# Gated linear attention feeding a two-layer MLP: weight rows read from their third byte on, top parts rebuilt by ScalarE alone, and a new hand-written order

## The chip, the cores and the metric

One core of one Trainium2 chip runs the whole program. The metric is the device time of one execution in microseconds, median over runs.

## The reference

```python
# 4 batches, 8 heads, 768 tokens, head size 48, float32
state = alpha[t] * state + k[t] (outer) v[t]        # per head, 48 x 48
y[t]  = q[t] @ state
# x = y as 3072 tokens x 384 (all heads side by side)
h  = x @ w_in                     # 384 x 2048, float64 weights
sp = log(1 + exp(h))              # softplus
g  = h * erf(sp)
out = g @ w_out                   # 2048 x 384, float64 weights
```

The weights come as float64, eight bytes each. All matrix products are made as sums of products of a high part and a low part of each operand, to keep the accuracy of float32.

## The kernel before, in words

**Order.** Everything is unrolled. The string `ORDER` (lines 30 to 132) lists about 1600 steps; a step's name is its kind and its indices. `Queue` (line 195) chains each engine's instructions in just that order, so every engine (TensorE is `pe`, VectorE `dve`, ScalarE `act`, SyncE `sp`, GpSimd `pool`) works its own steps strictly one after another. All loads and stores are issued by SyncE.

**Attention.** 24 chunks of 128 rows (64 tokens of two batches). Per chunk n: loads `la lk lq lv` (alpha, k, q, v), two scans on VectorE `sb sa` and a reciprocal `rc`, scaled keys and queries `kk qq`, on TensorE a transpose `pn`, scores `ps`, outputs `qt` and `sv` into the PSUM tile `py`, and the state update `pu`, with `mk td ta` on VectorE (`ta` on ScalarE for the first two chunks) and `ic kn` on ScalarE (`kd` is `kn` on VectorE). Then the chunk's result is split for the MLP: `xh` (ScalarE) writes the high part `x_hi`; the low part `x_lo` comes from `xl`, one VectorE subtraction, or from `xp` (TensorE subtracts the high part in PSUM) and `xe` (ScalarE copies).

**MLP.** 12 blocks of 256 tokens; block n takes chunks 2n and 2n+1. Four groups g of 512 hidden columns, each in two halves. `hm_n_g_half` is 18 matmuls (three terms, high times high first, then the low weights, then the low x), `he` (ScalarE) or `hd` (VectorE) copies its PSUM bank to the tile `hs`. Then on ScalarE `u`, `n1 n2 n3`, `g`, on VectorE `ma mb z1 z2`; `ga` (ScalarE) or `gd` (VectorE) makes the high part, `gl` (VectorE) the low part, and `om_n_g_half` is 12 matmuls into `acc`. `oe` (ScalarE) or `ob` (VectorE) copies `acc` out, `od` stores. `u` and `g` need another activation table than `n1 n2 n3`, so ScalarE loads a table at each change of kind along its order.

**Weights.** 12 tiles of `w_in` (`wli_0` to `wli_11`, 128 x 512; `hm` of group g needs tiles 3g to 3g+2) and 16 of `w_out` (`wlo_f`, 128 x 384; `om_n_g_half` needs f = 4g+2half and the next). Class `Weight` (lines 635 to 696) turns the eight bytes of a number into a float32: `wl` loads the row shifted by three bytes, so that one 32-bit word holds bytes 3 to 6 (`low`) and the lowest byte of the next word is byte 7, sign and upper exponent (`rest`). `wr` (VectorE) shifts that byte to the top of a float32 `top`; `wd` (ScalarE) writes it as float16 into the upper half of the same word, which moves the exponent; `wa` (VectorE) shifts `low` by 5 and ors it in, giving `z`. Then `wh` (ScalarE; `wk` is the same on VectorE) makes the high part `hi`, and the low part comes from `wq` (VectorE subtracts) or from `wp` and `we` (TensorE subtracts in a PSUM bank, ScalarE copies).

**Tiles.** `w_in` loads take the ring `hs` (7 tiles), `w_out` loads the ring `s` (6 tiles, line 187), which the MLP's `u` also uses; `top` and `z` lie together in the ring `w` (4 tiles). A ring's tile is taken again when its last reader is done. `dw_n` issues n dummy products of the identity into a spare PSUM bank (two matmul records each); the first `dw` also clears two banks with four short ones.

Of the kernel before, what the change touches and what calls it, by code (L numbers as in the profile page):

```python
# [35 lines left out]
wdi_5 wri_7 wdi_8 qq_2 whi_6 lk_2 ic_2 wli_9 wai_5 wdi_7 hm_0_0_0 whi_5 kk_2 wli_10 hm_0_0_1 ta_1 he_0_0_0 qt_2 ps_2
wai_7 wli_11 la_3 wqi_5 he_0_0_1 pn_2 whi_7 wlo_0 wqi_6 kn_2 wai_8 lk_3 lq_3 wri_9 lv_2 hm_0_1_1 whi_8 wri_10 u_0_0
sb_3 wqi_8 wri_11 rc_3 wqi_7 he_0_1_1 hm_0_1_0 he_0_1_0 sa_3 mk_2 kk_3 wdi_9 qq_3 hm_0_2_0 wlo_7 sv_2 ps_3 wdi_10
wdi_11 he_0_2_0 pu_2 xh_2 wai_9 wro_7 whi_9 wdo_7 wai_10 pn_3 lv_3 ic_3 wai_11 whi_10 la_4 whi_11 wqi_9 lq_4 xp_2 kn_3
n1_0_0 mk_3 lk_4 xe_2 wqi_10 n2_0_0 wqi_11 td_3 hm_0_2_1 he_0_2_1 sb_4 hm_0_3_1 wro_0 ta_2 wlo_4 rc_4 qt_3 wdo_0 kk_4  # L40
he_0_3_1 pu_3 n3_0_0 sa_4 sv_3 xh_3 ta_3 pn_4 wao_7 wlo_1 la_5 wro_1 lq_5 wlo_2 xl_3 hm_0_3_0 who_7 kn_4 wao_0 qq_4
wdo_1 ma_0_0 he_0_3_0 lk_5 wao_1 hm_1_0_1 u_0_1 mb_0_0 td_4 hm_1_1_1 he_1_0_1 g_0_0 who_0 lv_5 he_1_1_1 lv_4 hm_1_0_0
sb_5 ps_4 wqo_7 qt_4 ic_4 n1_0_1 wro_2 hm_1_1_0 z1_0_0 n2_0_1 wqo_0 rc_5 mk_4 he_1_0_0 z2_0_0 wro_4 sa_5 wdo_2 wdo_4
la_6 who_1 he_1_1_0 ic_5 kk_5 td_5 hm_1_2_0 wao_4 hm_1_3_0 wqo_1 lk_6 sv_4 n3_0_1 wlo_11 ga_0_0_0 qq_5 ma_0_1 wao_2
ga_0_0_1 gl_0_0_0 ps_5 mb_0_1 sb_6 wlo_5 pu_4 g_0_1 xh_4 ta_4 xp_4 gl_0_0_1 who_2 mk_5 z1_0_1 he_1_2_0 wlo_6 wqo_2
om_0_0_0 he_1_3_0 pn_5 xe_4 u_0_2 rc_6 wro_5 hm_1_3_1 kk_6 n1_0_2 who_4 kn_5 om_0_0_1 wro_6 lq_6 he_1_3_1 wlo_9 wdo_5
n2_0_2 wdo_6 pn_6 sa_6 z2_0_1 qt_5 qq_6 pu_5 n3_0_2 lk_7 ga_0_1_0 wao_5 sv_5 ps_6 ga_0_1_1 xh_5 td_6 kn_6 la_7 lv_6
who_5 wao_6 xp_5 wqo_4 ic_6 xe_5 hm_1_2_1 wro_11 wlo_8 ma_0_2 gl_0_1_1 wdo_11 wao_11 hm_2_1_0 wko_6 wqo_5 wlo_12
gl_0_1_0 u_0_3 u_1_0 wro_9 ta_5 g_0_2 om_0_1_0 he_1_2_1 wqo_6 lq_7 hm_2_1_1 n1_0_3 mb_0_2 sb_7 z1_0_2 wdo_9 rc_7 mk_6
z2_0_2 wao_9 he_2_1_1 he_2_1_0 who_11 ic_7 sa_7 wlo_13 ga_0_2_1 om_0_1_1 wro_12 ga_0_2_0 kk_7 hm_2_0_0 qq_7 wqo_11  # L50
# [25 lines left out]
he_5_1_0 pu_12 n2_4_2 g_3_3 ma_4_1 sv_12 pn_13 xh_12 z1_3_3 mb_4_1 he_5_0_0 om_3_0_1 z2_3_3 g_4_1 z1_4_1 hm_5_0_1
la_14 g_4_0 gd_3_3_1 kn_13 z1_4_0 he_5_0_1 om_3_0_0 gd_3_3_0 sb_14 gl_3_3_0 xl_12 ic_13 lk_15 u_5_0 lv_13 rc_14 ta_12
sa_14 od_2_1 gl_3_3_1 u_4_3 mk_13 hm_5_1_1 om_3_3_0 kk_14 he_5_1_1 u_5_1 n1_4_3 n3_4_2 z2_4_0 hm_5_3_0 n1_5_0 qq_14
la_15 ma_4_2 om_3_3_1 n2_4_3 sv_13 ps_14 he_5_3_0 n1_5_1 pu_13 mb_4_2 qt_13 oe_3_0 pn_14 n3_4_3 z2_4_1 td_14 ic_14
oe_3_1 ga_4_0_0 ta_13 n2_5_0 sb_15 gl_4_0_0 hm_5_3_1 kn_14 he_5_3_1 om_4_0_0 gd_4_1_1 hm_5_2_0 ga_4_0_1 lq_15 xh_13  # L80
kk_15 gl_4_1_1 g_4_2 td_15 n2_5_1 om_4_1_1 rc_15 gl_4_0_1 n3_5_0 hm_5_2_1 lv_15 he_5_2_0 he_5_2_1 od_3_0 xl_13
om_4_0_1 n3_5_1 ma_4_3 sa_15 mb_4_3 gd_4_1_0 qq_15 z1_4_2 hm_6_0_1 u_5_2 mk_14 g_4_3 gl_4_1_0 la_16 om_4_1_0 ma_5_0
hm_6_0_0 g_5_0 z2_4_2 qt_14 z1_4_3 ps_15 lv_14 lk_16 u_5_3 sb_16 n1_5_3 mb_5_0 pu_14 he_6_0_0 n2_5_3 gd_4_2_0 od_3_1
sv_14 hd_6_0_1 ic_15 pn_15 xh_14 gl_4_2_0 z2_4_3 om_4_2_0 u_6_0 ma_5_1 rc_16 gd_4_2_1 ga_4_3_0 kd_15 g_5_1 ic_16
hm_6_2_1 lq_16 gl_4_2_1 om_4_2_1 gl_4_3_0 ga_4_3_1 mb_5_1 n3_5_3 kk_16 hd_6_2_1 z1_5_0 hm_6_2_0 sa_16 om_4_3_0
# [838 lines left out]
```

## Time and profile before

| | us |
|---|---|
| median of 3 runs (514.16 to 514.84) | 514.84 |
| the profiled execution | 513.94 |
| its span | 512.2 |
| busy: TensorE / VectorE / ScalarE | 502.5 / 481.5 / 461.5 |
| first matmul of the MLP (`hm_0_0_0`) starts | 26.95 |
| `om_4_0_0` starts | 235.40 |
| end of the last matmul | 506.9 |

A matmul shown as busy may be waiting in TensorE's pipeline, so the order of starts, not the busy share, tells where it stands still. All of the program's instructions go through the helper on line 203; the profile tells them apart by tiles: `warm` is a `dw`, `h` the PSUM bank of `hm`, `pn` and `wp`, `acc` an `om`, `w` with `s` or `hs` a weight or the MLP's `w`.

### The profile page before, as it was taken

What the parts mean: (1) busy time and instruction counts of PE and PEld (TensorE: products, weight loads), DVE (VectorE), ACT (ScalarE), POOL (GpSimd) and SP (SyncE); (2) the same over time, 40 slices, a digit from 0 to 9 for tenths busy, and PEclk for the clock granted to TensorE, in tenths of its full rate; (3) what the DMA queues carried; (4) which work ended last, traced back from release to release, by engine and by line L of the source; (5) the groups of instructions that cost most, each with busy time, mean ns of one, the idle gap of its engine ahead of it and who ended that gap; (6) DMA issues with size and microseconds to landing.
All of it is one profiled execution on the core that took longest, in us unless ns stands there. A gap on an engine that the chain in (4) does not pass through costs nothing.

```text
span 512.2 us, 16809 instructions
## 1 busy us (share of the span) xinstructions
PE 502.5 (98%) x7438; PEld 478.4 (93%) x7438; DVE 481.5 (94%) x659; ACT 461.5 (90%) x615; POOL 5.6 (1%) x39
## 2 busy tenths in 40 slices
...
GB/s 304 397 236 148 134 208 118 202 27 51 101 21 135 44 65 58 64 58 66 93 23 136 85 22 59 58 23 100 42 60 98 20 23 32 2 1 32 0 32 34
DMA packets 21387, 43.69 MB, mean 85 GB/s; under 512 B 2368, under 2 KB 5440, under 8 KB 21312
## 3 DMA queue, kind: packets, MB, share of 16 engines
...
## 4 chain that ended last, share of the span: by engine, by line
PE 68%; ACT 24%; DVE 3%; issue 3%; DMA 1%; SPq 0%; ACTq 0%
PE acc L203 31%; PE h__112 L203 15%; PE h__113 L203 13%; PE py L203 4%; ACT L203 4%; PE both L203 3%; ACT w__101 L203 2%; ACT w__99 L203 2%; ACT s__85 L203 1%; PE warm L203 1%; ACT w__100 L203 1%; ACT s__89 L203 1%; ACT s__88 L203 1%; ACT s__90 L203 1%; DMA s__85<-in_moe_w_out_dram 1%
## 5 line engine op out<-in xcount | busy, mean ns | idle before, releaser
L203 ACT ACT_TABLE_LOAD x74 | 94.9, 1283 | 2.1 <-PEq L878 0.9
L203 PE MATMUL acc<-wo_hi,gh__103 128*128 128x384 f32 x192 | 43.7, 339 | 0.0
L203 PE MATMUL acc<-wo_hi,gl__105 128*128 128x384 f32 x192 | 43.4, 338 | 0.0
L203 PE MATMUL acc<-wo_lo,gh__103 128*128 128x384 f32 x192 | 43.2, 337 | 0.0
L203 PE MATMUL acc<-wo_hi,gh__102 128*128 128x384 f32 x192 | 43.1, 344 | 0.0
L203 PE MATMUL acc<-wo_hi,gl__104 128*128 128x384 f32 x192 | 41.5, 338 | 0.3 <-DVE gl__104 L203 0.3
L203 PE MATMUL acc<-wo_lo,gh__102 128*128 128x384 f32 x192 | 41.7, 338 | 0.0
L203 PEld LDWEIGHTS acc<-wo_hi,gl__104 128*128 128x128 f32 x192 | 34.2, 188 | 0.7 <-DVE gl__104 L203 0.7
L203 PEld LDWEIGHTS acc<-wo_hi,gl__105 128*128 128x128 f32 x192 | 34.4, 188 | 0.0
L203 PEld LDWEIGHTS acc<-wo_lo,gh__103 128*128 128x128 f32 x192 | 34.4, 188 | 0.0
L203 PEld LDWEIGHTS acc<-wo_lo,gh__102 128*128 128x128 f32 x192 | 34.3, 188 | 0.0
L203 DVE TENSOR_TENSOR_SCAN B<-raw_a,back 128x520 f32<-128x520 f32 x24 | 29.7, 1238 | 3.8 <-DMA raw_a<-in_alpha_dram 3.7
L203 PEld LDWEIGHTS acc<-wo_hi,gh__102 128*128 128x128 f32 x192 | 31.5, 188 | 0.9 <-ACT gh__102 L203 0.4
L203 PEld LDWEIGHTS acc<-wo_hi,gh__103 128*128 128x128 f32 x192 | 31.9, 188 | 0.2
L203 DVE TENSOR_TENSOR_SCAN A<-raw_a,start 128x520 f32<-128x520 f32 x24 | 29.7, 1237 | 0.1
L203 PE MATMUL h__112<-x_hi__109,wi_hi 128*128 128x256 f32 x150 | 22.2, 283 | 0.0
L203 PE MATMUL h__112<-x_hi__108,wi_lo 128*128 128x256 f32 x150 | 22.0, 281 | 0.1
L203 PE MATMUL h__112<-x_hi__108,wi_hi 128*128 128x256 f32 x150 | 22.1, 283 | 0.0
L203 PE MATMUL h__112<-x_hi__109,wi_lo 128*128 128x256 f32 x150 | 21.8, 281 | 0.0
L203 PE MATMUL h__112<-x_lo__110,wi_hi 128*128 128x256 f32 x150 | 21.8, 281 | 0.0
L203 PE MATMUL h__112<-x_lo__111,wi_hi 128*128 128x256 f32 x150 | 21.7, 280 | 0.0
L203 ACT ACTIVATE w__98<-w__98 128x1024 f32<-128x1024 f32 (+2 forms) x19 | 16.8, 885 | 4.5 <-DVE w__98 L203 4.4
...
## 6 DMA issues: line engine op xcount, KB each, us to landing
...
out_dram<-o__107 SPq DMA_DIRECT2D x12, 192.0 KB, 3.3
s__86<-in_moe_w_out_dram SPq DMA_DIRECT2D x4, 384.0 KB, 5.3
```

Source lines behind the costliest of these rows:

```text
L203: ins = made(*args, **kw)
```

## The change

- A weight row is loaded shifted by two bytes. The word `low` then holds bytes 2 to 5, and bytes 6 and 7 are a bfloat16 number of their own, read with a step of eight bytes.
- `wr` is gone (28 VectorE instructions). `wd` reads that bfloat16 and writes the float16 into the upper half of one of two tiles `top`, cleared once by VectorE at the start. `wa` shifts by 13 and takes its `z` tile only now.
- The numbers come out smaller by 2^8: `he`, `hd`, `oe` and `ob` multiply by 2^8. `hd` so becomes a multiplication where it was a copy.
- The ring `s` has 5 tiles.
- The order is another one. What it issues of each kind, where that differs:

| steps | before | after |
|---|---|---|
| dummies in all `dw` | 12 | 7 |
| `wp` and `we` | 4 | 2 |
| `wq` | 24 | 26 |
| `wh` / `wk` | 27 / 1 | 23 / 5 |
| `xp` and `xe` / `xl` | 6 / 18 | 4 / 20 |
| `he` / `hd` | 72 / 24 | 76 / 20 |
| `ga` / `gd` | 55 / 41 | 49 / 47 |
| `kn` / `kd` | 17 / 5 | 19 / 3 |
| `oe` / `ob` | 17 / 7 | 15 / 9 |
| table loads by the order of `u`, `n`, `g` | 73 | 77 |

```diff
 ORDER = """
-la_0 sb_0 wli_3 rc_0 lk_0 sa_0 dw_1 wri_3 wdi_3 wlo_3 dw_1 lq_0 kk_0 wro_3 wai_3 wlo_10 dw_2 pn_0 wdo_3 kn_0 qq_0
-whi_3 wao_3 wro_10 ps_0 wli_1 wdo_10 dw_8 who_3 la_1 wqi_3 mk_0 ic_0 wli_4 wao_10 sb_1 wli_0 wri_1 lv_0 lk_1 rc_1
-wri_4 wpo_3 sa_1 lq_1 sv_0 wri_0 wdi_1 wdi_4 who_10 weo_3 pu_0 wai_4 kk_1 qq_1 xh_0 wdi_0 pn_1 ic_1 wqo_10 whi_4 wai_1
...
+la_0 sb_0 rc_0 wli_2 dw_4 sa_0 lk_0 wli_1 lq_0 wli_3 wdi_2 wai_2 kk_0 lv_0 qq_0 wdi_1 ic_0 whi_2 ps_0 wai_1 dw_1 mk_0
+sv_0 wdi_3 pn_0 whi_1 wai_3 wpi_2 la_1 wli_4 xh_0 sb_1 rc_1 xp_0 dw_1 lk_1 kn_0 wdi_4 lq_1 xe_0 wli_0 sa_1 kk_1 wei_2
+whi_3 pn_1 qq_1 wqi_1 wai_4 lv_1 pu_0 wlo_3 wdi_0 ps_1 kn_1 whi_4 dw_1 mk_1 ta_0 sv_1 wli_5 pu_1 wdo_3 wai_0 whi_0
+wqi_3 wdi_5 xh_1 la_2 ta_1 wao_3 wqi_4 wpi_0 ic_1 wei_0 xp_1 wli_7 sb_2 xe_1 wlo_10 who_3 lq_2 wai_5 rc_2 td_2 wdi_7
+sa_2 wai_7 whi_5 hm_0_0_0 qq_2 hm_0_0_1 wli_6 qt_2 lk_2 ic_2 wdo_10 wli_8 wli_9 wao_10 he_0_0_0 kk_2 la_3 lv_2 wdi_6
...
-    keep_s = Ring(keep, s=(grp, F32, NG + 2))
+    keep_s = Ring(keep, s=(grp, F32, NG + 1))
...
+    tops = Ring(keep, top=([P, 512], F32, 2))
+    for t in tops.tiles["top"]:
+        nc.vector.memset(t, 0.0)
...
-            copy(self.hs[g][:, sl], self.phs.pop((g, half)))
+            copy(self.hs[g][:, sl], self.phs.pop((g, half)), 2.0**8 if w_in.dtype != F32 else 1.0)
...
-            copy(o, self.acc[c][:, :DM], RT2)
+            copy(o, self.acc[c][:, :DM], RT2 * 2.0**8 if w_out.dtype != F32 else RT2)
...
-                self.src = src.bitcast(U8)[:, 8 * c * n + 3 : 8 * (c + 1) * n + 3]
+                self.src = src.bitcast(U8)[:, 8 * c * n + 2 : 8 * (c + 1) * n + 2]
...
-                self.low, self.rest = st[:, :, 0], st[:, :, 1]
+                self.low = st[:, :, 0]
+                self.high = flat.bitcast(BF16).rearrange("p (n four) -> p n four", four=4)[:, :, 2]
...
-        def wr(self):
-            if self.wide:
-                buf = keep_w.tile([P, 2, 512], F32, name="wbuf", tag="w")
-                self.top, self.z = buf[:, 0, : self.n], buf[:, 1, : self.n]
-                dve.tensor_scalar(
-                    out=self.top.bitcast(I32), in0=self.rest, scalar1=24, scalar2=None, op0=ALU.logical_shift_left
-                )
-
         def wd(self):
             if self.wide:
-                high = self.top.bitcast(F16).rearrange("p (n two) -> p n two", two=2)[:, :, 1]
-                act.activation(high, self.top, AF.Copy)
+                self.top = tops.tile([P, 512], F32, name="top", tag="top")[:, : self.n]
+                half = self.top.bitcast(F16).rearrange("p (n two) -> p n two", two=2)[:, :, 1]
+                act.activation(half, self.high, AF.Copy, scale=0.5)
 
         def wa(self):
             if self.wide:
+                self.z = keep_w.tile([P, 2, 512], F32, name="wbuf", tag="w")[:, 1, : self.n]
                 dve.scalar_tensor_tensor(
-                    out=self.z.bitcast(I32), in0=self.low, scalar=5, in1=self.top.bitcast(I32),
+                    out=self.z.bitcast(I32), in0=self.low, scalar=13, in1=self.top.bitcast(I32),
                     op0=ALU.logical_shift_right, op1=ALU.bitwise_or,
                 )
```

## Rows read from the trace of the kernel before

**Rows 1.** Busy us by stretch: PE, PEld, DVE, ACT, POOL; clock, DMA share, GB/s.

```profile
0.00:26.95 26.95, 23.49 (x308) 12.89 (x309) 18.34 (x34) 14.45 (x30) 3.46 (x17) 1.00 0.94 344
26.95:235.40 208.45, 207.46 (x3610) 200.09 (x3609) 206.08 (x291) 202.00 (x294) 1.18 (x12) 1.00 0.33 103
235.40:506.90 271.50, 271.50 (x3524) 265.41 (x3522) 257.13 (x337) 244.59 (x292) 0.98 (x10) 1.00 0.15 46
```

**Rows 2.** The chain that ended last, in time order: start us, us, what.

```profile
180.88 2.12 PE acc L203 x12
...
489.46 17.48 PE acc L203 x96
```

**Rows 3.** Timeline of TensorE up to `hm_0_0_0`: start us, us, instructions, [idle before].

```profile
1.87 2.08 PE L203 MATMUL warm<-ident 128*128 128x512 f32 x2 [1.87 <-POOL ident masks.py:199]
...
5.32 2.74 PE L203 MATMUL warm<-ident 128*128 128x512 f32 x6
...
9.83 7.13 PE L203 MATMUL warm<-ident 128*128 128x512 f32 x16
...
26.65 0.47 PE L203 MATMUL py<-x_hi__108,minus 128*128 128x192 f32 x2 [0.20 <-ACT x_hi__108 L203]
26.95 0.89 PE L203 MATMUL h__112<-x_hi__108,wi_hi 128*128 128x256 f32 x6
```

**Rows 4.** What VectorE waited for: us in total, times, longest.

```profile
DVE sT L203 <- ACT T L203: 4.6, 1, 4.6
DVE B L203 <- DMA raw_a<-in_alpha_dram: 3.7, 1, 3.7
```

**Rows 5.** Timeline of VectorE in the head.

```profile
9.53 0.35 DVE L203 TENSOR_SCALAR w__100<-s__86 128x384 int32<-128x384 int32 x1
9.80 0.69 DVE L203 TENSOR_TENSOR wi_lo<-w__98,wi_hi 128x512 fp32r<-128x512 f32 x1
10.40 0.68 DVE L203 TENSOR_TENSOR sT<-both,mask 128x512 f32<-128x512 f32 x1
...
14.50 0.40 DVE L203 TENSOR_SCALAR w__99<-hs__94 128x512 int32<-128x512 int32 x1
14.81 0.69 DVE L203 SCALAR_TENSOR_TENSOR w__98<-hs__93,w__98 128x512 int32<-128x512 int32 x1
```

**Rows 6.** Groups of instructions by form: busy us, mean ns of one, idle before.

```profile
L203 DVE TENSOR_TENSOR s__88<-s__88,w__100 128x1024 f32<-128x1024 f32 x4 | 4.9, 1220 | 0.2 <-ACT s__88 L203 0.2
...
L203 DVE TENSOR_SCALAR o__107<-acc 128x384 f32<-128x384 f32 x4 | 2.2, 554 | 0.2 <-PE acc L203 0.2
...
L203 DVE COPY hs__92<-h__113 128x512 f32<-128x512 f32 x3 | 2.1, 689 | 0.1
```

**Rows 7.** Timeline of ScalarE: in the head, and at a table load.

```profile
20.71 0.62 ACT L203 ACTIVATE wi_hi<-w__101 128x512 fp32r<-128x512 f32 x1
21.23 0.77 ACT L203 ACTIVATE w__100<-w__100 128x512 f16<-128x512 f32 x1
21.86 0.47 ACT L203 ACTIVATE x_lo__110<-py 128x384 fp32r<-128x384 f32 x1
...
44.13 1.28 ACT L203 ACT_TABLE_LOAD   x1
45.42 1.06 ACT L203 ACTIVATE s__88<-s__88 128x1024 f32<-128x1024 f32 x1
```

**Rows 8.** DMA issues: KB each, median us from issue to landing.

```profile
s__86<-in_moe_w_out_dram SPq DMA_DIRECT2D x4, 384.0 KB, 5.3
...
hs__95<-in_moe_w_in_dram SPq DMA_DIRECT2D x1, 512.0 KB, 7.6
...
hs__91<-in_moe_w_in_dram SPq DMA_DIRECT2D x1, 512.0 KB, 3.9
```

**Rows 9.** Timeline of SyncE: the issue of `wli_3` and of `wli_2`.

```profile
1.35 0.42 SPq L203 DMA_DIRECT2D hs__91<-in_moe_w_in_dram  x1
...
9.37 0.59 SPq L203 DMA_DIRECT2D hs__95<-in_moe_w_in_dram  x1
```

More of the change, by code (lines that the diff above doesn't have):

```diff
@@ L30 @@
 ORDER = """
-la_0 sb_0 wli_3 rc_0 lk_0 sa_0 dw_1 wri_3 wdi_3 wlo_3 dw_1 lq_0 kk_0 wro_3 wai_3 wlo_10 dw_2 pn_0 wdo_3 kn_0 qq_0
-whi_3 wao_3 wro_10 ps_0 wli_1 wdo_10 dw_8 who_3 la_1 wqi_3 mk_0 ic_0 wli_4 wao_10 sb_1 wli_0 wri_1 lv_0 lk_1 rc_1
-wri_4 wpo_3 sa_1 lq_1 sv_0 wri_0 wdi_1 wdi_4 who_10 weo_3 pu_0 wai_4 kk_1 qq_1 xh_0 wdi_0 pn_1 ic_1 wqo_10 whi_4 wai_1
-wli_2 kn_1 wri_2 whi_1 wli_6 xp_0 lv_1 wdi_2 ps_1 xe_0 ta_0 mk_1 la_2 wpi_4 wli_5 wpi_1 wri_6 wai_0 lq_2 wei_4 sv_1
-whi_0 wai_2 sb_2 wri_5 whi_2 pu_1 rc_2 td_2 wei_1 xh_1 wpi_2 wei_2 xp_1 wli_8 wqi_0 xe_1 sa_2 wri_8 wdi_6 wli_7 wai_6
@@ L36 @@
[L36 to L50, printed above, removed]
@@ L76 @@
[L76 to L85, printed above, removed]
@@ new lines @@
+n2_0_3 sa_7 lv_6 ga_0_2_1 kk_7 n2_1_0 om_0_2_0 gl_0_2_1 n3_0_3 qq_7 n3_1_0 wqo_11 he_2_1_0 qt_6 ps_7 he_2_0_1 who_15
+ma_0_3 la_8 pu_6 g_0_3 wao_12 mb_0_3 ta_6 ma_1_0 sv_6 pn_7 wdo_13 hm_2_0_0 z1_0_3 wlo_14 kn_7 om_0_2_1 he_2_0_0
+hm_2_2_1 u_1_1 hm_2_2_0 xh_6 wko_12 z2_0_3 td_7 g_1_0 ga_0_3_0 wqo_15 wdo_14 ic_7 wao_13 xl_6 who_13 wao_14 mk_7
+ga_0_3_1 sv_7 who_14 pu_7 gl_0_3_1 lq_8 u_1_3 u_1_2 wqo_13 sb_8 gl_0_3_0 mb_1_0 qt_7 kk_8 he_2_2_1 wqo_12 he_2_2_0
+n1_1_2 xh_7 rc_8 hm_2_3_1 wqo_14 z1_1_0 n1_1_1 sa_8 lk_9 n2_1_1 om_0_3_1 td_8 ic_8 n3_1_1 qq_8 xl_7 n2_1_2 om_0_3_0
@@ new lines @@
+lq_9 oe_0_0 z2_1_0 ma_1_1 ga_1_0_0 qt_8 oe_0_1 lv_9 ga_1_0_1 la_9 gl_1_0_0 ps_8 g_1_1 pn_8 om_1_0_0 gl_1_0_1 sb_9
+he_2_3_1 lv_8 n3_1_2 kn_8 lk_10 mb_1_1 kk_9 rc_9 z1_1_1 n1_1_3 om_1_0_1 hm_2_3_0 z2_1_1 ga_1_1_0 he_2_3_0 n2_1_3
+ma_1_2 n3_1_3 ga_1_1_1 g_1_2 gl_1_1_0 mb_1_2 sa_9 hm_3_1_0 hm_3_1_1 la_10 gl_1_1_1 ta_7 qq_9 ma_1_3 u_2_1 mk_8
+he_3_1_1 om_1_1_1 om_1_1_0 he_3_1_0 z1_1_2 z2_1_2 td_9 gd_1_2_1 sv_8 ps_9 sb_10 g_1_3 pu_8 pn_9 gl_1_2_1 u_2_0
+ga_1_2_0 od_0_1 gl_1_2_0 mb_1_3 lq_10 od_0_0 u_2_2 n1_2_2 mk_9 ic_9 z1_1_3 kd_9 rc_10 n1_2_0 hm_3_2_1 om_1_2_0 n1_2_1
```

155 lines of the change are left out of this document (84 added, 71 removed).

## The prediction, made before the changed kernel ran

> **What bounds the kernel now.** I read three views first. The stretches [rows 1] cut the execution at two starts: the first MLP matmul (`hm_0_0_0`, 26.95) and `om_4_0_0` (235.40). In the head DMA is nearly full (share 0.94) while ScalarE works 14.45 of 26.95 us and VectorE 18.34. From 26.95 to 235.40 all three engines are full at once: idle are 208.45 - 206.08 = 2.4 us of VectorE and 208.45 - 202.00 = 6.4 of ScalarE, and TensorE shows almost none. From 235.40 on VectorE has 14 us and ScalarE 27 us to spare, TensorE none. The chain that ended last [rows 2] says the same at its end: matmuls alone, 12 in 2.12 us and the last 96 in 17.48. So the time is a head, a stretch in which VectorE paces (least idle off TensorE), and a TensorE stretch of fixed work.
>
> The timeline of TensorE [rows 3] shows the head: dummies (16 records from 9.83, 0.43 us each), then real work whose inputs come late, and `hm_0_0_0` at 26.95. VectorE's waits [rows 4] give its idle time: 3.7 us for the first alpha and 4.6 us for `ta_0` on ScalarE, which itself came late behind the dummies: 8.3 of the 26.95 - 18.34 = 8.6 us idle in the head.
>
> **The change, part by part.**
>
> *VectorE work.* 28 `wr` go. One takes 14.81 - 14.50 = 0.31 us (512 columns) or 9.80 - 9.53 = 0.27 (384) from start to start [rows 5]: 12 x 0.31 + 16 x 0.27 = 8.0 us. I counted in both orders what stands on VectorE up to the low part that lets TensorE into block 4 (before `gl_4_0_0` for `om_4_0_0`, after `gl_4_0_1` for `om_4_0_1`). A step costs its duration less the 0.09 by which neighbours overlap (0.69 long, 10.40 - 9.80 = 0.60 apart [rows 5]). Added there: 5 `wk` instead of 1 (4 x 0.3 = 1.2), one `wq` more of each size (0.60 and 0.47, 1.1), 2 `xl` and 1 `ob`, each 384 columns from PSUM (0.55 - 0.09 [rows 6], 1.4), 2 `hd` (0.60 each, 1.2), and by the order 1 `z1`, 1 `z2`, 1 `gl` less 1 `ta`: 2 x (1.22 - 0.09) [rows 6] + 0.60 - 0.46 = 2.4. Sum -8.0 + 7.3 = -0.7 us. At that point the new order has one `om` less still to do on TensorE: -2.1 us [rows 2]. For `wk`, a cast within SBUF, bounds are 0.27 (the `wr` of 384) and 0.60 (the two-source `wq`); I take 0.3, as `wr` also has one SBUF source, and the other end is 4 x 0.3 = 1.2 us more.
>
> *`hd` and `oe`, `ob` with a factor.* `ob` already multiplies: 554 ns for 384 columns; `hd` copies 512 in 689 [rows 6]. The difference, 135 ns for 128 columns, is 1.05 ns a column, the rate of both; so zero for `hd`. On ScalarE the factor is an operand that `oe` has already. Zero.
>
> *`wd`.* It now reads a bfloat16 every eight bytes. Rows: 21.86 - 21.23 = 0.63 us with float16 out, against 21.23 - 20.71 = 0.52 for the float32 cast `wh` [rows 7]. Low end: as `wh`, 28 x -0.1 = -3 us of ScalarE. High end, if the reading step costs a second pass over 512 columns: 28 x 0.4 = +12 us. I take 0.63, since the output, by which the two rows differ, stays what it was. The two `top` tiles: each `wd` waits for the `wa` two before it, which the order has ahead of it everywhere; clearing them is hidden by the 3.7 us that VectorE waits for alpha anyway.
>
> *ScalarE.* Four `wh` go to VectorE (0.52 for the large one [rows 7], less for the three of 384: -1.8), two `we` (-1.0) and two `xe` (-0.7) are gone; four table loads are new. A load occupies 45.42 - 44.13 = 1.29 us and the next instruction starts at once [rows 7]: +5.2. Net before block 4 about +1.7 with 6.4 us idle in that stretch to cover it: zero.
>
> The Trainium skill's page "ScalarE: Activation LUTs", section "What ACT_TABLE_LOAD costs", adds to the 1283 ns of a load a drain of about 1380. Four loads would then be 10.6 us, an estimate from that page; the rows show no such drain before or after the load, so the sum stays without it.
>
> *The head.* Bytes decide when weights land. `wli_3` was issued at 1.35 and took 3.9 us, landing at 5.25 with 772 KB issued in all; `wli_2` was issued at 9.37, 7.6 us, landing at 16.97 with 5129 KB [rows 8, 9]: (5129 - 772) / 11.72 = 372 KB/us. In the new order `wli_0`, last of the three tiles of group 0, ends 4361 KB: 5.25 + 3589/372 = 14.9. `wli_5` ends 5513 KB: 18.0. On ScalarE `wdi_5` stands ahead of `xh_1`, so `xh_1` starts at 18.0 + 0.65 and takes 0.4; then `xp_1` (26.95 - 26.65 = 0.30 [rows 3]), and `hm_0_0_0` at 19.5. VectorE agrees: up to and with `wai_0` it has 12.5 us of work from 3.7 on, with about 1.2 us of waits for q and a top part: 17.4, then `whi_0`, `wp`, `we`: the low weights at 20.2, which `hm_0_0_0` wants 0.7 us after its start. I take 19.7, that is -7.25. TensorE's own work in the head falls by 5 dummies of 0.86 (4.3 us) and two `wp` (1.3); that is what makes room. VectorE idle in the head: 3.7 + 1.2 = 4.9 instead of 8.6, -3.7. The new loads wait at no other place: the second alpha still needs `sa_0`, as before.
>
> *The sum.* By TensorE: -7.25, and two `xp` less (2 x 0.30): -7.85, if what it loses later stays. By VectorE: -3.7 - 0.7 - 2.1 = -6.5. The smaller gain decides, as VectorE paces until block 4; after it TensorE's work is the same, as is the tail (512.2 - 506.9 = 5.3). The profiled execution took 513.94, so it would be 507.4; the median of before is 0.9 above it, and 514.84 - 6.5 gives 508.3 us, the forecast.
>
> **The rivals.**
>
> *The later waits go too.* From `hm_0_0_0` to the last matmul TensorE takes 480 us; its steps there, each at the spacing that its kind has where nothing is late (`om` 2.12 [rows 2], the other kinds likewise from the timeline), make about 471. If half of the 9 us vanishes: 508.3 - 4.5 = 504. For it: 8.0 us of `wr` are gone from the weight phase. Against: VectorE's sum to block 4 falls by 0.7 only.
>
> *Top parts dearer.* The high end of `wd`, +12 us of ScalarE, less its 6.4 idle: 508.3 + 5.6 = 513.9. Against: the rows' fixed output. Nothing in the trace has that input, so it can't be excluded. This is also the case in which the change does not do what it says: ScalarE gives back what VectorE saves.
>
> *The clock.* The first two dummy records took 1.04 us each (1.2 GHz), from 5.32 on 0.43 (2.4 GHz) [rows 3], after TensorE had worked without a break from 1.87; the granted clock then stays 1.00 [rows 1]. With 5 dummies fewer there are more gaps: from about 8.0 to 8.6 and before each of `sv_0`, `pn_1`, `sv_1`. If it fell back to 1.2 GHz the 4.4 us of attention work and two `wp` in the head and two or three `hm` would double, +4 to +7 after what is hidden: 513 to 514. The Trainium skill's page "TensorE: Matmul & The Clock Gate", section "HAM oscillation — how this bites in real kernels", has the clock halved by idle gaps; that speaks against this change. The 1.3 us between `pn_0` and `ps_0` in the trace did not do it.
>
> *Slower: five tiles in ring `s`.* 12 of 16 `w_out` loads must wait for a tile, where 11 did. By the sums of both orders five of them have 5.1 to 5.6 us from the tile's release to their `wd`; a landing takes 5.3 at 384 KB [rows 8] and 7.6 for 512 KB under load. If five are late by 2 us each, ScalarE stands (its steps are in order), VectorE's `wa` behind it, and 10 us go: 518. It turns the gain into a loss from 6.5 / 5 = 1.3 us late in each place, that is, loads of about 6.7 us. Against: DMA's share is 0.33 in this stretch [rows 1].
>
> **How the numbers follow.** A measurement of this kernel tells about 0.2%, 1.0 us, from no change. Forecast (505 to 511.5): 0.64. Later waits gone (below 505): 0.12. Dear top parts 0.08, clock 0.05, each half within 0.2% and half just faster. Late loads: 0.11, of which 0.06 slower and the rest a smaller gain. So faster 0.87, same 0.07, slower 0.06. The range leaves out the slow tail and the very best: 504.0 to 512.5.
>
> **What would show it.** Right: `hm_0_0_0` between 19 and 20.5; dummies 14 records; no TENSOR_SCALAR on `w`; VectorE's idle in the head near 5 us; `om_4_0_1` near 229; TensorE without a gap from there; `wd` 0.77 us long. Wrong: `wd` over 0.9 us; matmuls of 1.04 us after 6 us; ScalarE waiting for `in_moe_w_out_dram` between 45 and 100 us; TensorE waiting for `gh` or `gl` after block 4.

## The result, and the profile after

| | before | after |
|---|---|---|
| median, us (4 runs each) | 514.68 | 506.97 (506.65 to 507.52) |
| ratio, 95% interval | | 0.9853 [0.9836, 0.9870] |
| profiled execution; its span | 513.94; 512.2 | 507.52; 505.7 |
| `hm_0_0_0` starts | 26.95 | 21.34 |
| end of the last matmul | 506.9 | 501.49 |
| from there to the end of the span | 5.3 | 4.2 |
| busy: TensorE / VectorE / ScalarE | 502.5 / 481.5 / 461.5 | 495.0 / 478.3 / 463.0 |

The changed kernel is 7.7 us faster by the medians (6.7 to 8.4 by the interval), 6.4 by the profiled executions; the forecast was 508.3. The table says where the 6.5 us of span went: the MLP starts 5.6 us earlier, and after the last matmul another 1.1 us are gone. Between them nothing changed: 480.15 us from `hm_0_0_0` to the last matmul's end, where it was 506.9 - 26.95 = 480.0. The profiled execution of the changed kernel is the slowest of its four; the others' spans are 504.9 to 505.4.

One number below needs a remark: of the five executions of the kernel with four dummies two, at 517.06 and 515.26 us, are left out of its ratio; their granted clock was 0.986 on the mean, against 0.996 to 1.000 in the other three.

The stretches of the changed kernel, cut at `hm_0_0_0` and `om_4_0_0` as in [rows 1], with the first 13 us of the MLP apart:

```profile
0.00:21.34 21.34, 17.15 (x292) 9.54 (x293) 16.60 (x24) 13.31 (x26) 3.46 (x17) 1.00 0.92 336
21.34:34.57 13.23, 13.01 (x305) 12.16 (x303) 12.94 (x22) 13.05 (x27) 0.10 (x1) 1.00 1.02 372
...
21.34:230.48 209.14, 207.03 (x3606) 199.89 (x3605) 206.74 (x286) 202.92 (x291) 1.19 (x12) 1.00 0.35 113
230.48:501.49 271.01, 270.81 (x3524) 264.15 (x3522) 254.38 (x335) 246.76 (x295) 1.54 (x10) 1.00 0.15 46
```

VectorE's idle time in the head is 21.34 - 16.60 = 4.7 us (8.6 before). Between 21.34 and 34.57 nothing has room: VectorE is idle for 0.3 us, ScalarE for 0.2, TensorE for 0.2, and the DMA engines are full (share 1.02). The last stretch is TensorE's alone, and the chain that ended last ends in `om` again (answers to [rows 2]):

```profile
471.43 12.48 PE acc L204 x72
484.02 6.75 PE acc L204 x36
492.20 9.30 PE acc L204 x52
```

The head on TensorE (answers to [rows 3]), and its one long stop soon after:

```profile
1.87 5.64 PE L204 MATMUL warm<-ident 128*128 128x512 f32 x8 [1.87 <-POOL ident masks.py:199]
7.35 0.81 PE L204 MATMUL both<-T,ident 128*128 128x192 f32 x4
9.79 0.69 PE L204 MATMUL both<-raw_q,raw_k 48*64 48x64 f32 x32 [1.63 <-DVE raw_q L204]
10.42 1.12 PE L204 MATMUL warm<-ident 128*128 128x512 f32 x2
...
21.04 0.47 PE L204 MATMUL py<-x_hi__111,minus 128*128 128x192 f32 x2 [0.41 <-ACT x_hi__111 L204]
21.34 0.89 PE L204 MATMUL h__115<-x_hi__111,wi_hi 128*128 128x256 f32 x6
...
35.38 0.39 PE L204 MATMUL h__116<-x_hi__111,wi_lo 128*128 128x256 f32 x2
36.90 0.63 PE L204 MATMUL h__116<-x_hi__111,wi_lo 128*128 128x256 f32 x4 [1.13 <-issue]
```

There are 14 dummy records: eight at the start, then three pairs between the attention products. `hm_0_0_0` comes 0.30 after `xp_1`, as before, and `xp_1` is what waits: for ScalarE's `x_hi`. ScalarE and SyncE say why (answers to [rows 7] and [rows 9]):

```profile
19.00 0.60 ACT L204 ACTIVATE wi_hi<-w__97 128x512 fp32r<-128x512 f32 x1
19.78 0.79 ACT L204 ACTIVATE top__101<-hs__95 128x512 f16<-128x512 bf16 x1 [0.17 <-DMA hs__95<-in_moe_w_in_dram]
20.43 0.47 ACT L204 ACTIVATE x_hi__111<-py 128x384 fp32r<-128x384 f32 x1
...
44.81 1.28 ACT L204 ACT_TABLE_LOAD   x1
46.11 1.06 ACT L204 ACTIVATE s__87<-s__87 128x1024 f32<-128x1024 f32 x1
```

```profile
11.12 0.33 SPq L204 DMA_DIRECT2D hs__95<-in_moe_w_in_dram  x1
```

`hs__95` is `wli_5`. ScalarE's wait for it ended at 19.78, 8.7 us after its issue, and `xh_1` stands behind its `wdi_5`. The wait itself is 0.17 us: until 19.60 ScalarE was at `whi_0`, the step ahead. The new `wd` takes 0.79 and 0.65 from start to start (20.43 - 19.78), the old one 0.77 and 0.63 [rows 7]. The next instruction begins 46.11 - 44.81 = 1.30 us after the table load began, as before. By the Trainium skill's page "ScalarE: Activation LUTs", section "What ACT_TABLE_LOAD costs", some 1380 ns of drain would come on top of a load; this kernel does not show it either.

VectorE at the start, and the two kinds of copy that now multiply (answers to [rows 4] to [rows 6]):

```profile
1.06 0.48 DVE L190 MEMSET top__101<- 128x512 f32 x1 [1.06 <-PEq L874]
1.60 0.48 DVE L190 MEMSET top__102<- 128x512 f32 x1
3.73 1.24 DVE L204 TENSOR_TENSOR_SCAN B<-raw_a,back 128x520 f32<-128x520 f32 x1 [1.64 <-DMA raw_a<-in_alpha_dram]
```

```profile
L204 DVE TENSOR_SCALAR o__109<-acc 128x384 f32<-128x384 f32 x6 | 3.3, 547 | 0.0
...
L204 DVE TENSOR_SCALAR hs__93<-h__116 128x512 f32<-128x512 f32 x4 | 2.7, 682 | 0.3 <-PE h__116 L204 0.3
```

The two clearings lie inside the wait for alpha, and `hd` with its factor takes 682 ns where the plain copy took 689 [rows 6]. DMA (answers to [rows 8]), and the last figure of a stretch, GB/s, from the landing of `wli_3` in the kernel before to that of `wli_2` there, and to that of `wli_5` in the changed kernel:

```profile
s__85<-in_moe_w_out_dram SPq DMA_DIRECT2D x5, 384.0 KB, 5.6
...
hs__95<-in_moe_w_in_dram SPq DMA_DIRECT2D x2, 512.0 KB, 8.1
```

```profile
5.25:16.97 11.72, 11.02 (x60) 5.40 (x60) 11.54 (x21) 5.22 (x10) 0.00 (x0) 1.00 1.02 389
5.25:19.78 14.53, 12.62 (x285) 7.54 (x284) 12.67 (x19) 10.16 (x20) 0.00 (x0) 1.00 1.03 390
```

### The profile page after: what moved, and what is told of

The parts are those of the page before. It is cut to its first block, busy times and chain, and to the rows that moved or that the text cites. A ratio compares the mean times of both kernels' runs of the same rounds, so it can differ in the third digit from the quotient of the medians.

```text
span 505.7 us, 16774 instructions
## 1 busy us (share of the span) xinstructions
PE 495.0 (98%) x7418; PEld 473.6 (94%) x7418; DVE 478.3 (95%) x643; ACT 463.0 (92%) x609; POOL 6.2 (1%) x39
## 4 chain that ended last, share of the span: by engine, by line
PE 41%; DVE 9%; ACT 8%; issue 2%; DMA 0%; DVEq 0%
PE acc L204 21%; PE h__116 L204 9%; PE h__115 L204 8%; PE py L204 2%; ACT L204 2%; PE both L204 2%; DVE t L204 1%; ACT w__100 L204 1%; ACT s__85 L204 1%; DVE A L204 1%; DVE gl__108 L204 1%; ACT s__89 L204 1%; ACT s__86 L204 1%; ACT w__99 L204 1%; DVE gl__107 L204 1%
## 5 line engine op out<-in xcount | busy, mean ns | idle before, releaser
L204 PE MATMUL acc<-wo_hi,gl__108 128*128 128x384 f32 x192 | 43.4, 338 | 0.1
L204 PE MATMUL acc<-wo_hi,gh__106 128*128 128x384 f32 x192 | 43.0, 337 | 0.0
L204 PE MATMUL acc<-wo_hi,gh__105 128*128 128x384 f32 x192 | 42.2, 339 | 0.0
L204 PE MATMUL acc<-wo_hi,gl__107 128*128 128x384 f32 x192 | 41.3, 336 | 0.0
L204 PE MATMUL h__115<-x_hi__112,wi_hi 128*128 128x256 f32 x156 | 23.4, 285 | 0.0
L204 ACT ACTIVATE s__87<-s__87 128x1024 f32<-128x1024 f32 x22 | 23.2, 1054 | 0.1
L204 PE MATMUL h__116<-x_hi__111,wi_hi 128*128 128x256 f32 x150 | 22.7, 287 | 0.0
L204 PE MATMUL h__115<-x_lo__114,wi_hi 128*128 128x256 f32 x156 | 22.6, 280 | 0.0
L204 PE MATMUL h__116<-x_lo__113,wi_hi 128*128 128x256 f32 x150 | 21.8, 281 | 0.0
```

The source lines that it names most:

```text
L204: ins = made(*args, **kw)
```

## The experiments

Two theories at first. **V**: the time came from the VectorE work that is gone, as the prediction had it (VectorE paces until block 4). **H**: it came from the earlier start of the MLP, which TensorE then carries to the end.

**1. The new path in the old order.** The changed kernel's code with `ORDER` of before, less its 28 `wr` (of the edit, the two rings).

```diff
-    keep_s = Ring(keep, s=(grp, F32, NG + 1))
+    keep_s = Ring(keep, s=(grp, F32, NG + 2))
...
-                self.top = tops.tile([P, 512], F32, name="top", tag="top")[:, : self.n]
+                buf = keep_w.tile([P, 2, 512], F32, name="wbuf", tag="w")
+                self.top, self.z = buf[:, 0, : self.n], buf[:, 1, : self.n]
```

> The old order with the new weight path: no wr, wd from bfloat16, factors 2^8; six tiles in ring s and the tops in the first halves of the w tiles, as before (left out: the lower halves of those words are cleared only once, so later weights carry stray low bits). Theory V (VectorE paces up to block 4): 8.1 us of VectorE work are gone, so the time falls until ScalarE or the head takes over, 2 to 5 us below before. Rival H (the start of the first MLP matmul sets the end, TensorE alone afterwards): the head is held by the eight dummies as before, the first MLP matmul stays at 26 to 27 us and the time within 1 us of before.

Measured: 514.00 us, ratio 0.9994 [0.9985, 1.0003]. Its stretches, cut at the same starts:

```profile
0.00:27.30 27.30, 24.65 (x309) 13.47 (x309) 18.02 (x29) 14.31 (x30) 3.46 (x17) 1.00 0.92 341
27.30:235.56 208.26, 207.12 (x3610) 199.94 (x3609) 200.64 (x271) 201.71 (x294) 1.18 (x12) 1.00 0.32 103
```

VectorE does 206.08 - 200.64 = 5.4 us less [rows 1] in a stretch that is 0.2 us shorter. In this order VectorE does not pace, although it was idle for only 2.4 us of it before; TensorE is idle for 1.1. V falls as a statement on that stretch, and the path alone is worth nothing. Whether ScalarE's chain of steps holds parts of the stretch was not tried.

**2. Seven dummies in the kernel before.** `dw_8` becomes `dw_3`.

```diff
-whi_3 wao_3 wro_10 ps_0 wli_1 wdo_10 dw_8 who_3 la_1 wqi_3 mk_0 ic_0 wli_4 wao_10 sb_1 wli_0 wri_1 lv_0 lk_1 rc_1
+whi_3 wao_3 wro_10 ps_0 wli_1 wdo_10 dw_3 who_3 la_1 wqi_3 mk_0 ic_0 wli_4 wao_10 sb_1 wli_0 wri_1 lv_0 lk_1 rc_1
```

> The kernel before with dw_8 made dw_3: seven dummies, as many as after the change, everything else as before. If the dummies hold the head: sv_0, ta_0 and the second mk come up to 4.3 us earlier, VectorE's wait of 4.6 us goes, first MLP matmul at 23 to 24 us, time 2.5 to 4.5 us below before under V and H alike. Rival (the weights' landing holds the head): the first MLP matmul within 1 us of 26.95 and the time within 1 us of before.

Measured: 513.86 us, ratio 1.0000 [0.9981, 1.0019]. In the profile `hm_0_0_0` starts at 24.08, 2.9 us earlier, and `om_4_0_0` at 232.11 (235.40 before), so the gain is carried for 350 us. TensorE's timeline near 375 shows where it goes:

```profile
374.48 0.42 PE L203 MATMUL py<-sT,raw_v__114 64*32 64x64 f32 x22
376.50 0.67 PE L203 MATMUL py<-sT,raw_v__114 64*32 64x64 f32 x42 [1.60 <-issue]
377.09 1.07 PE L203 MATMUL h__113<-x_hi__109,wi_hi 128*128 128x256 f32 x6
377.96 1.48 PE L203 MATMUL h__113<-x_hi__109,wi_lo 128*128 128x256 f32 x6
```

TensorE stops for 1.6 us in the middle of one `sv`, waiting for no tile ("issue"), and six `hm` matmuls, 0.87 us elsewhere, then take 1.48: the granted clock is at 1.2 GHz from 377.8 to 381.2. Step by step against the trace of before, TensorE is 2.3 us ahead at 346, 0.5 ahead behind the stop, and 1.0 behind after the low clock; its last matmul ends at 507.95, later than before. This execution took 514.99, 1.1 us over the median, with a granted clock of 0.995 on the mean against 0.997 in the median one; even without the low clock the forecast of 2.5 to 4.5 us would have been missed. A third theory, **C**, comes from here: TensorE stopped for its own code. That comes in packets of 16 KB on the instruction queue (59 in this kernel as in the changed one), and one was in flight from 373.8 to 375.0, the stop beginning at 374.9.

**3. Seven dummies again, stores swapped too**, to see whether the stop comes back. Beside the edit of 2:

```diff
-om_11_3_1 oe_11_1 ob_11_0 od_11_1 od_11_0
+om_11_3_1 oe_11_1 ob_11_0 od_11_0 od_11_1
```

> The kernel before with seven dummies (dw_3 for dw_8) and its last two stores exchanged. Theory C (the 3 us that fewer dummies win in the head are lost again late, where TensorE stands while its code is fetched): first MLP matmul near 24, om_6_0_0 near 317, then a stop of over 1 us that the profile calls issue, at the same place as before (sv_20) or near it, time 0.5 to 1.5 us below before. Rival (that stop was a chance of one execution): no stop over 0.7 us after 40 us, last matmul near 504, time 3 to 4 us below before.

Measured: 513.24 us, ratio 0.9978 [0.9969, 0.9987]; `hm_0_0_0` at 25.25 in the profile.

```profile
375.56 0.42 PE L203 MATMUL py<-sT,raw_v__114 64*32 64x64 f32 x22
377.58 0.67 PE L203 MATMUL py<-sT,raw_v__114 64*32 64x64 f32 x42 [1.60 <-issue]
```

The same stop between the same two matmuls, again at a code packet (374.8 to 376.2, the stop from 376.0); the traces of before, of 1 and of 11, whose TensorE works the same steps with twelve dummies, have no such stop there. So the stop belongs to a place in TensorE's code, as C has it, though that it waits for the code itself is not shown by an experiment (more on it in the last section). The clock did not fall this time, and the 1.1 us gained lie in C's 0.5 to 1.5, though `hm_0_0_0` was to come near 24.

**4. Twelve dummies in the changed order.**

```diff
-whi_3 pn_1 qq_1 wqi_1 wai_4 lv_1 pu_0 wlo_3 wdi_0 ps_1 kn_1 whi_4 dw_1 mk_1 ta_0 sv_1 wli_5 pu_1 wdo_3 wai_0 whi_0
+whi_3 pn_1 qq_1 wqi_1 wai_4 lv_1 pu_0 wlo_3 wdi_0 ps_1 kn_1 whi_4 dw_6 mk_1 ta_0 sv_1 wli_5 pu_1 wdo_3 wai_0 whi_0
```

> The changed kernel with twelve dummies as before the change: the last dw_1 is dw_6, ahead of sv_1. H: first MLP matmul 3 to 4.3 us later, time 3 to 4 us above the changed kernel. V: VectorE loses as much where it waits for the second chunk (about 3 us), the same 2.5 to 4 us. If the dummies don't matter (as in the kernel before, where taking five out changed the time by 0.5 us): within 1 us of the changed kernel.

Measured: 512.82 us, ratio 0.9970 [0.9957, 0.9983], 5.85 over the changed kernel. `hm_0_0_0` starts at 25.97 (+4.6; forecast were 3 to 4.3) and nothing is made good: the last matmul ends at 507.76 (+6.3), with two stops that wait for no tile, 1.30 us at 34.9 and 1.06 at 40.4, where the changed kernel has 0.22 and 1.13.

```profile
17.94 5.42 PE L204 MATMUL warm<-ident 128*128 128x512 f32 x12
...
25.97 0.90 PE L204 MATMUL h__115<-x_hi__111,wi_hi 128*128 128x256 f32 x6
```

The five added dummies, 10 of these 12 records, stand on the path with their whole 10 x 0.43 = 4.3 us. (This profile also has the clock at 0.50 from 11.54 to 14.96, after TensorE had stood still for 2.24 us at 9.85, where the changed kernel waits 1.63; that is ahead of the added dummies, and the execution is 0.85 us over the median.) So in the changed order the dummies cost what they last; in the old one [rows 3] leaving out five brought 2.9 us in the head, of which a stop later took most.

**5. The old path in the changed order.** `wr` again, just ahead of each `wd`, on one of the two `top` tiles; rows from the fourth byte, no factors.

```diff
+        def wr(self):
+            if self.wide:
+                self.top = tops.tile([P, 512], F32, name="top", tag="top")[:, : self.n]
+                dve.tensor_scalar(
+                    out=self.top.bitcast(I32), in0=self.rest, scalar1=24, scalar2=None, op0=ALU.logical_shift_left
+                )
...
-                act.activation(half, self.high, AF.Copy, scale=0.5)
+                act.activation(half, self.top, AF.Copy)
```

> The new order with the old weight path: rows shifted by three bytes, a wr on VectorE just ahead of each wd, no factors; tops and rings as after the change. If the order is what counts and the path only room on VectorE: 9 to 14 us above the changed kernel (the idle shifts cost 10.9, and here wd waits for VectorE too), that is, slower than before. Rival (the order alone carries the gain): within 2 us of the changed kernel.

Measured: 529.44 us, ratio 1.0289 [1.0275, 1.0303]: 22.5 over the changed kernel. `hm_0_0_0` starts at 24.14, `om_1_0_0` at 133.21 (111.17 after). The stretch between, and ScalarE's waits:

```profile
24.14:133.21 109.07, 96.12 (x1793) 90.72 (x1791) 96.07 (x158) 89.78 (x145) 0.78 (x7) 0.94 0.45 145
```

```profile
ACT top__101 L206 <- DVE top__101 L206: 18.1, 11, 4.4
ACT top__102 L206 <- DVE top__102 L206: 10.1, 9, 2.3
```

All three engines stand idle, TensorE and VectorE for 13.0 us each, ScalarE for 19.3: over the whole execution ScalarE waits 28 us for `wr`, VectorE in places for ScalarE's `wd` (2.3 us at 45.75, the longest), and the clock falls (0.94 on the mean). That is far more than the 8 us of work. The direction was expected, the size not (9 to 14). With 1 it says: the path alone brings nothing, and this order without it loses. Only one place for `wr` was tried, just ahead of each `wd`; part of the 22.5 us may be that place, and an order made for the old path could do better.

**6. Idle shifts in the changed kernel**: one VectorE shift into `z` ahead of each `wa`, 28 in all, the work of the old `wr` without its place in the chain to ScalarE.

```diff
+                dve.tensor_scalar(
+                    out=self.z.bitcast(I32), in0=self.low, scalar1=24, scalar2=None, op0=ALU.logical_shift_left
+                )
```

> The changed kernel with an idle shift (the old wr's operation, into the z tile) ahead of each of the 28 wa, 8.1 us of VectorE work. Theory V: 5 to 8 us slower than the changed kernel, 512 to 515, spread over the stretch up to block 4. Rival H: only the five shifts ahead of the first MLP matmul count, at most 1.6 us, 507 to 508.6.

Measured: 517.85 us, ratio 1.0068 [1.0054, 1.0081], 10.9 over the changed kernel. `hm_0_0_0` moves by 0.3 only, `hm_0_2_0` by 3.5 (38.12), `om_1_0_0` by 10.7 (121.83):

```profile
21.64:38.12 16.48, 14.62 (x305) 13.82 (x303) 15.89 (x28) 13.87 (x27) 0.10 (x1) 0.90 0.98 351
38.12:121.83 83.71, 77.25 (x1493) 72.64 (x1488) 82.08 (x133) 75.88 (x119) 0.59 (x6) 1.00 0.39 127
```

VectorE is the fullest engine in both, and all that is added to it comes out as time, and more: 10.9 us for 8.1 us of work, where V had 5 to 8 and H at most 1.6. Part of the rest is the clock, at 0.50 from 29.7 to 33.1. In the changed order VectorE has no slack for more work while weights are made.

**7. Less VectorE work after the weights' first phase**: `ma` and `mb` of blocks 0 and 1 on half the columns (the edit of `ma`; `mb` likewise).

```diff
-            dve.tensor_tensor(out=self.t, in0=self.s[g], in1=self.w[g], op=ALU.mult)
+            c = 512 if isinstance(self.tok, int) and self.tok < 512 else 1024
+            dve.tensor_tensor(out=self.t[:, :c], in0=self.s[g][:, :c], in1=self.w[g][:, :c], op=ALU.mult)
```

> The changed kernel with ma and mb of blocks 0 and 1 on half of the columns (left out: the second half of these 16 operations), 8.5 us of VectorE work less between 40 and 120 us. V: 3 to 8 us below the changed kernel. H: within 0.6 us of it, since TensorE has no waits there that VectorE causes; VectorE idles 8 us more.

Measured: 507.26 us, ratio 0.9857 [0.9841, 0.9873]: as the changed kernel. The stretch to 160 us, here and in the changed kernel:

```profile
21.34:160.00 138.66, 137.09 (x2504) 131.83 (x2503) 129.74 (x197) 136.76 (x207) 0.88 (x9) 1.00 0.40 132
```

```profile
21.34:160.00 138.66, 137.31 (x2505) 131.98 (x2504) 137.36 (x197) 136.83 (x209) 0.89 (x9) 1.00 0.41 132
```

7.6 us less of VectorE's work and the same starts to within 0.3 us. With 6: as the kernel stands VectorE is just full enough not to hold TensorE up; more work on it costs, less gives nothing.

**8 and 9. The wait for `wli_5` taken off `xh_1`.** In 8 `wdi_5` moves behind `xe_1`; in 9 also `qq_2` ahead of `wai_7`, as in 8 TensorE lost its lead at `qt_2`, which needs `qq_2` (it ended at 25.52 there).

```diff
-wqi_3 wdi_5 xh_1 la_2 ta_1 wao_3 wqi_4 wpi_0 ic_1 wei_0 xp_1 wli_7 sb_2 xe_1 wlo_10 who_3 lq_2 wai_5 rc_2 td_2 wdi_7
-sa_2 wai_7 whi_5 hm_0_0_0 qq_2 hm_0_0_1 wli_6 qt_2 lk_2 ic_2 wdo_10 wli_8 wli_9 wao_10 he_0_0_0 kk_2 la_3 lv_2 wdi_6
+wqi_3 xh_1 la_2 ta_1 wao_3 wqi_4 wpi_0 ic_1 wei_0 xp_1 wli_7 sb_2 xe_1 wdi_5 wlo_10 who_3 lq_2 wai_5 rc_2 td_2 wdi_7
+sa_2 qq_2 wai_7 whi_5 hm_0_0_0 hm_0_0_1 wli_6 qt_2 lk_2 ic_2 wdo_10 wli_8 wli_9 wao_10 he_0_0_0 kk_2 la_3 lv_2 wdi_6
```

> The changed kernel with one step moved: wdi_5, which waited for its load until 19.78, stands behind xe_1 on ScalarE, so that xh_1 need not wait for it. Theory H (TensorE runs without waits from the first MLP matmul on, so its start sets the end): first MLP matmul near 20.0 instead of 21.34, time 1 to 1.4 us below the changed kernel. Theory V (in the new order VectorE has no slack in the weight phase, as the idle shifts showed): the first MLP matmul comes earlier, but TensorE waits as much later, time within 0.4 us of the changed kernel.

> The changed kernel with wdi_5 behind xe_1 and qq_2 ahead of wai_7 on VectorE, since qt_2 waited for qq_2 after the first MLP matmuls had come earlier. If the next gate is weight tile 7 and the code stop at hm_0_2_0: qt_2 0.6 us earlier and lost again there, 506.5 to 507.4. If qq_2 was the gate: 0.6 to 1.1 us below the changed kernel, 505.9 to 506.4.

Measured: 507.26 us, ratio 0.9859 [0.9843, 0.9875], and 507.17, 0.9856 [0.9841, 0.9871]: no gain. `hm_0_0_0` starts at 20.27 and 20.72, 1.07 and 0.62 earlier, but `hm_0_2_0` at 34.62 and 35.21 (34.57 after). TensorE in 8, then the stretch in 9 with a wait of VectorE and one of ScalarE:

```profile
23.87 0.87 PE L204 MATMUL h__116<-x_lo__113,wi_hi 128*128 128x256 f32 x6
25.63 1.02 PE L204 MATMUL py<-raw_q,T 48*32 48x64 f32 x64 [0.89 <-PE h__116 L204]
```

```profile
20.72:35.21 14.49, 13.45 (x305) 12.37 (x303) 13.57 (x22) 13.28 (x25) 0.10 (x1) 1.00 0.99 359
...
22.41 0.69 DVE L204 SCALAR_TENSOR_TENSOR w__99<-hs__95,top__101 128x512 int32<-128x512 int32 x1 [0.76 <-ACT top__101 L204]
...
26.16 0.79 ACT L204 ACTIVATE top__102<-hs__90 128x512 f16<-128x512 bf16 x1 [1.18 <-DVE w__100 L204]
```

The start of the MLP can still be moved, but neither move brought forward what follows it at 35 us. In the changed kernel all three engines and the DMA engines are full up to there (the result's second stretch); in 9 VectorE is idle for 0.9 us of it and ScalarE for 1.2, as `wdi_5`, put later, now holds VectorE, and `wai_7`, put behind `qq_2`, holds ScalarE. H needs that limit: the head's gain counts up to where this phase lets it pass.

**10. Four dummies in the changed order**: the three `dw_1` are left out (one of the three lines).

```diff
-sv_0 wdi_3 pn_0 whi_1 wai_3 wpi_2 la_1 wli_4 xh_0 sb_1 rc_1 xp_0 dw_1 lk_1 kn_0 wdi_4 lq_1 xe_0 wli_0 sa_1 kk_1 wei_2
+sv_0 wdi_3 pn_0 whi_1 wai_3 wpi_2 la_1 wli_4 xh_0 sb_1 rc_1 xp_0 lk_1 kn_0 wdi_4 lq_1 xe_0 wli_0 sa_1 kk_1 wei_2
```

> The changed kernel with its first four dummies only (three dw_1 left out). If the clock needs them: matmuls of the head after 8 us or of the first MLP steps at 1.2 GHz in the record, first MLP matmul 1 to 3 us later, time 1 to 3 us above the changed kernel. If not: clock 2.4 GHz throughout, first MLP matmul within 0.4 us of 21.34 since a load holds it, time within 0.5 us.

Measured: ratio 0.9865 [0.9845, 0.9884], `hm_0_0_0` at 21.11: nothing gained. In the profiled execution (506.67 us) the clock stays at 1.00 and TensorE runs through `hm_0_2_0` without its stop. Whether the three pairs keep the clock up in every execution (the remark in the result) is open.

**11 and 12. The last two stores.** In the kernel before, `od_11_1` stands ahead of `od_11_0`; in the changed one it is the other way round. 11 swaps them in the kernel before, 12 in the changed one.

```diff
-om_11_3_1 oe_11_1 ob_11_0 od_11_1 od_11_0
+om_11_3_1 oe_11_1 ob_11_0 od_11_0 od_11_1
```

```diff
-ga_11_3_1 gl_11_3_0 od_10_0 gl_11_3_1 om_11_3_0 om_11_3_1 oe_11_0 ob_11_1 od_11_0 od_11_1
+ga_11_3_1 gl_11_3_0 od_10_0 gl_11_3_1 om_11_3_0 om_11_3_1 oe_11_0 ob_11_1 od_11_1 od_11_0
```

> The kernel before with its last two stores exchanged, so that the half copied first is stored first, as the changed order does. If the store order makes the shorter tail: the end comes 0.4 to 1.1 us earlier after the last matmul and the time falls by as much. Rival (the tail differs by chance of the DMA): within 0.3 us of before, tail 5.0 to 5.4 us.

> The changed kernel with its last two stores in the order of the kernel before: od_11_1 ahead of od_11_0. Theory S (the tail is 1.1 us shorter because the half that is copied first is also stored first): od_11_1 waits for its copy, which begins at 501.53, and is issued near 502.1 as now; od_11_0 follows some 0.4 us later, near 502.5 instead of 501.0. The tail after the last matmul grows from 4.2 to 4.6-5.0 us, the median to 507.4-507.8, a ratio to the changed kernel of 1.001 to 1.0016. Rival (the shorter tail comes from something else, such as the kinds of copies at the end): the tail stays 4.2, the median 507.0. The milestones ahead of the last matmul stay within 0.3 us by both.

Measured: 513.84 us, ratio 0.9987 [0.9978, 0.9996], and 508.50, 0.9889 [0.9872, 0.9905], that is 1.5 over the changed kernel. The end of the timeline in the kernel before, in the changed one, and in 12:

```profile
506.96 0.49 ACT L203 ACTIVATE o__107<-acc 128x384 f32<-128x384 f32 x1 [4.60 <-PE acc L203]
507.48 0.34 SPq L203 DMA_DIRECT2D out_dram<-o__107  x1
507.91 0.39 SPq L203 DMA_DIRECT2D out_dram<-o__106  x1
```

```profile
501.00 0.34 SPq L204 DMA_DIRECT2D out_dram<-o__109  x1
501.53 0.56 DVE L204 TENSOR_SCALAR o__110<-acc 128x384 f32<-128x384 f32 x1 [3.40 <-PE acc L204]
502.12 0.33 SPq L204 DMA_DIRECT2D out_dram<-o__110  x1
```

```profile
501.70 0.34 SPq L204 DMA_DIRECT2D out_dram<-o__110  x1
502.13 0.38 SPq L204 DMA_DIRECT2D out_dram<-o__109  x1
```

The half that is copied first waits in SyncE's order behind the other's copy unless it is stored first. In 12 the last matmul ends at 501.08, 0.41 earlier than in the changed kernel, and the last issue stands at 502.1 in both: 1.05 us after the last matmul in 12, 0.62 in the changed kernel. From there the span takes 4.5 us in 12 and 3.6 in the changed kernel: two stores issued 0.43 apart end later than two that are 1.12 apart. So the tail is 506.6 - 501.1 = 5.5 us against 4.2 (forecast were 4.6 to 5.0, which counted the later issue alone), and the store order accounts for the 1.1 us; in the kernel before it gave less, 4.5 instead of 5.3.

## Why the prediction was right, and where it was not

The time (508.3 forecast, 506.97 measured), the range and the direction hold. The steps:

- **The price of `wd`** taken at 0.63 us from start to start: 0.65. Neither end of its range (-3, +12) came, and the rival of dear top parts is out.
- **Factors at nothing, clearings hidden, `wr` gone**: as predicted (682 against 689 ns; both clearings before 2.1 us, alpha used from 3.73 as before).
- **Table loads at 1.29 us and hidden**: the duration is right (1.30). That they are hidden was not tried by itself; 6.2 us of ScalarE's time are idle between 21.34 and 230.48.
- **VectorE's idle time in the head**, 4.9 forecast: 4.7 up to `hm_0_0_0`. Its work up to `om_4_0_0` fell by 1.1 us (16.60 + 206.74 against 18.34 + 206.08), 0.7 forecast. These two terms of VectorE's sum were sound; what they were used for was not, below.
- **`hm_0_0_0` at 19.7 (-7.25)**: 21.34 (-5.6), outside its 19 to 20.5; `om_4_0_1` came at 232.6 where 229 was named. The path was right, `wdi_5`, `xh_1`, `xp_1` (its steps add up to 19.35, not 19.5); its first term was not, for two reasons. ScalarE's own work in the head was not summed: `whi_0`, ahead of `wdi_5`, ran from 19.00 to 19.60, so with `wli_5` there at 18.0 `wdi_5` could have begun only some 0.25 us earlier (an estimate: 19.00 and the 0.52 of a `wh` [rows 7]), and in 8, without `wdi_5` in the way, `hm_0_0_0` still came at 20.27. And `wli_5` came at 19.78 instead of 18.0 with the DMA engines as fast as before, 390 against 389 GB/s (the result's last rows): the sum counted only the bytes issued up to it, (5513 - 772) KB, but by the rate some 0.8 MB more moved until 19.78 (390 x 14.53 less those bytes), from loads issued behind it.
- **"The smaller gain decides, as VectorE paces until block 4"**: the step that failed, though the time came out. Experiment 1 took 5.4 us of VectorE's work out of that stretch in the old order and 7 took 7.6 out in the changed one, and nothing moved. An idle time of 2.4 us in 208 [rows 1] was read as the mark of the engine that paces; it only showed that the order keeps it nearly as full as TensorE. From the start of the MLP to about 35 us VectorE does limit, in a chain with ScalarE and with the DMA engines full (8, 9), and with more work it limits up to block 1 too (6). So the term that counts is TensorE's, which the prediction had worked out as -7.85 and set aside.
- **The two `xp` less, -0.6**: given back. `hm_0_0_0` to the last matmul took 0.15 us more, and one stop of 1.13 us at 35.8 to 36.9 is more than what they saved. It is shorter in other executions of the same TensorE code (0.58 in 12).
- **The tail at nothing**: -1.1, by the order of two stores (12). The prediction named the tail "the same" without looking at its last steps.
- **The rivals.** The later waits stayed (480 us). The clock was 1.00 from 5.8 us to the end of the work, so that rival did not come in this execution; it was near, as in 4 a stop of 2.24 us in place of 1.63 at the same product was followed by it. (The prediction's 1.3 us between `pn_0` and `ps_0` run from start to start; TensorE stood still for 0.70 of them, against 1.63 in the changed kernel.) Five tiles in ring `s` were enough: no wait of ScalarE for `in_moe_w_out_dram` between 45 and 100 us.

That -6.5 by VectorE and -6.5 of span agree is partly luck: by TensorE it is -5.6 + 0.15 - 1.1, a smaller head gain than computed and a tail that was not counted.

That neither part does it alone is seen from the pairs: against the kernel before in the same runs, the path in the old order -0.3 us (its interval holds a ratio of 1), seven dummies in the old order -0.5 (likewise), the changed order with the old path +15.1 (with `wr` in one place only), with the new path and twelve dummies -1.5; together -7.7. The reading that fits them: the path frees VectorE and takes one link out of the chain to ScalarE while weights are made, and the order spends that on an earlier first MLP matmul. What share of the 7.7 us each has can't be told, as an order was not made for the old path with seven dummies.

No kernel tried beats the changed one by what a measurement can tell.
